# The tail of a fused attention, MLP and mixture kernel issued from one written plan, with its maximum and low halves on other engines

## The chip, the cores and the metric

The kernel runs on one core of one Trainium2 chip. The metric is the device time in microseconds (us), the median of several executions. The core's engines work side by side, each through its own queue in order, and wait for one another by semaphores: TensorE (PE, matrix products), VectorE (DVE), ScalarE (ACT), GpSimd (POOL) and SyncE (SP, which here only issues DMAs).

## The reference

```python
# attention: b=4, 8 heads, 576 rows, head size 64; phi(x) = [exp(xW-m), exp(m-xW)]
kv = einsum(phi(k), v);  x = (phi(q) @ kv) / (phi(q) @ sum(phi(k)) + 1e-6)   # -> x: 2304 x 512
# MLP, 512 -> 2048 -> 512
h = np.maximum(x @ w_in, 0.0)
x = h * h @ w_out
# mixture, E=4 experts, 512 -> 1024 -> 512
p = domain_probs / (domain_probs.sum(-1, keepdims=True) + 1e-09)
for e in range(E):
    h = np.maximum(x @ w1[e], 0.0)
    out += p[:, e:e + 1] * (h @ w2[e])
```

All is computed to float32 accuracy. TensorE multiplies in a shorter format, so each operand is split into a high half (a rounded copy) and a low half (the operand minus its high half), and each product is three matmuls: high by low, low by high, high by high.

## The kernel before, in words

The 2304 tokens are cut by batch row b into blocks of 512 tokens; the 64 tokens left over of each of the four rows make one block of 256, the rest.

The first part is issued from a written plan: functions put steps into a list with `at(time, ...)`, and the list, sorted by time, sets the order of every engine's queue. The times only order; nothing waits for a clock. It computes attention for all rows, and the MLP for rows 0 and 1 (`Unit`, lines 515 and 562 on PE). Attention's outputs for rows 2, 3 and the rest go to DRAM (`put_x`, `put_rest`).

The second part, from line 723 on, here the tail, is written as ordinary code without a plan, and the framework orders it. Its three passes are the MLP on rows 2, 3 and the rest (8 groups of hidden features), the mixture on rows 0 and 1 (16 groups), and the mixture on rows 2, 3 and the rest (16 groups). One group of a pass is a unit:

- `Weights` loads 256 columns of the first matrix (`f`) and 256 rows of the second (`f2`), forms four sums of blocks on POOL (line 801), and splits all into high halves on ACT and low halves on POOL (line 83).
- `hidden_pair` computes the hidden activations of two blocks with seven block products in place of eight (Strassen's scheme): px, py, pz and pv are PSUM banks, and DVE combines them into u4, c and u2 (line 868). Each product is 6 matmuls of 512 columns (line 860), 42 in all.
- `act_mlp` or `act_mix` turns the four hidden tiles (px, u4, c, u2) into a high half gh and a low half gl. In a mixture, ACT writes gh = relu. For px, in PSUM, DVE forms gl as max(px, 0) - gh in one instruction (line 845). For the other three, in SBUF, POOL first takes the maximum in place (line 849) and then subtracts (line 83).
- `hidden_rest`, in passes with the rest, adds 24 matmuls of 256 columns (line 897) into one bank pa.
- `out_mlp` or `out_mix` computes the outputs: 8 banks pa of 6 matmuls of 512 columns (line 912 or 929); for the rest 4 banks of 6 matmuls of 256 columns in the MLP, 2 of 6 by 512 in a mixture. DVE adds each bank to the accumulators `x2` (line 917 or 935).

`flush` puts the outputs of a unit behind the next unit's seven products in the pass without a rest, and behind the unit's own `hidden_rest` in the others. `Operands` prepares a pass's left operands: four sums or differences on DVE (T3, T1, T2, T4) and seven splits. Their low halves are named ol.

Of the kernel before, what the change touches and what calls it, by code (L numbers as in the profile page):

```python
# [21 lines left out]
def fused_kernel(  # L22
# [44 lines left out]
    actx = ExitStack()  # L67
# [37 lines left out]
    def load_probs():  # L105
# [22 lines left out]
        "g": actx.enter_context(tc.tile_pool(name="g", bufs=4)),  # L128
        "w": actx.enter_context(tc.tile_pool(name="w", bufs=3, side="right")),
    }  # L130
    xpool = actx.enter_context(tc.tile_pool(name="x", bufs=2))
# [440 lines left out]
    def new_x2(b):  # L572
        n = MAIN if b < B else NL
        pool = ypool if b < 2 else zpool
        x2[b] = pool.tile([P, KD, n], F32, name=f"x2_{b}")
# [140 lines left out]
    with tc.manual_schedule():  # L716
        for _, _, fn, args in sorted(plan, key=lambda x: x[:2]):
            fn(*args)
    cctx.close()
    actx.close()  # L720


    def left(name, bufs=1):
        return ctx.enter_context(tc.tile_pool(name=name, bufs=bufs, reuse_waits="tile"))

    ps_t = ctx.enter_context(tc.tile_pool(name="ps_t", bufs=4, space=bass.MemoryType.PSUM, reuse_waits="tile"))
    pools["ps"] = ps_t
    w2pool = left("w2", 2)
    gpool = left("g2", 6)
    upool = left("sums", 6)  # L730
    opool = left("operands")
    zpool = left("z")
    fpool = left("f", 4)
    w1pool = left("w1", 2)
    lpool = left("rest")

    def f_tile(*shape):
        return fpool.tile([P, *shape], F32, tag="f", name="f")

    def u_tile():  # L740
        return upool.tile([P, 512], F32, tag="u", name="u")

    for b in (2, 3, 4):
        new_x2(b)

    HK = KD // 2
    PRODUCTS = ("B11", "T2", "T1", "T3", "B21", "B22", "T4")

    class Operands:


        def __init__(self, b0, b1, engs):
            (b11, b12), (b21, b22) = ([x2[b][:, k : k + HK] for b in (b0, b1)] for k in (0, HK))
            self.h, self.l = {}, {}
            t = {"B11": b11, "B21": b21, "B22": b22, "T1": b12}
            for name, a, b in (("T3", b22, b12), ("T1", b12, b11), ("T2", b22, "T1"), ("T4", b21, "T2")):
                if name not in t:
                    t[name] = f_tile(HK, MAIN)
                sub(nc.vector, t[name], a, t.get(b, b) if isinstance(b, str) else b)
            for name, eng in zip(PRODUCTS, engs):  # L760
                self.h[name], self.l[name] = (
                    opool.tile([P, HK, MAIN], F32R, tag=x + name, name=f"o{x}") for x in "hl"
                )
                split(nc.scalar, eng, self.h[name], self.l[name], t[name])

    def load_x():
        for b in (2, 3):
            for k in range(0, KD, HK):
                nc.sync.dma_start(out=x2[b][:, k : k + HK], in_=kept["x", b][:, k : k + HK])
        nc.sync.dma_start(out=x2[B], in_=kept["xL"])  # L770

    class Rest:


        def __init__(self):
            self.h, self.l = (lpool.tile([P, KD, NL], F32R, tag=f"rest{n}", name="rest") for n in "hl")
            split(nc.scalar, nc.vector, self.h, self.l, x2[B])
# [3 lines left out]
    FIRST_OF = ((1, 2), (0, 3))  # L781

    class Weights:
        def __init__(self, first_srcs, second_srcs, rest):
            w1 = w1pool.tile([P, 2, 8, HK, P], F32R, tag="w1", name="w1")
            self.h, self.l = h, l = w1[:, 0], w1[:, 1]
# [4 lines left out]
            for s in (0, 1):  # L791
                nc.sync.dma_start(out=f[:, 3 * s], in_=first_srcs[1][:, s * HK : (s + 1) * HK])
# [216 lines left out]
```

## Time and profile before

| what | value |
|---|---|
| median of 3 runs | 1495.78 us (1494.72 to 1496.09) |
| the profiled execution's own time | 1497.08 us |
| its span, first to last instruction | 1495.3 us |
| busy, share of the span | PE 93%, POOL 69%, DVE 59%, ACT 39% |
| PE from 460.8 us on | 976.6 us busy in 1029.6 us |
| median against the profiled execution's own time | 1.30 us less |

All engines run through the whole span, so the busiest one, PE, is the one to ask first. A busy PE is not a PE at its peak: the granted clock (1.00 is 2.4 GHz, 0.50 is 1.2 GHz) stands beside its busy time in the windows below.

### The profile page before, as it was taken

The page shows a single profiled execution, that of the slowest core. Times are in us where ns is not written, and L with a number is a line of the kernel's source. Part 1 is how long each engine was busy: PE and PEld are TensorE (multiplying, and loading weights), DVE is VectorE, ACT ScalarE, POOL GpSimd, SP SyncE. Part 2 cuts the span into 40 slices and gives each one's busy share as a digit, 9 for nine tenths or more (in the row PEclk, how much of TensorE's full clock was granted, in tenths as well). Part 3 has the DMA queues.
Part 4 walks back from the last instruction along what each step waited for, and adds up shares of the span by engine and source line. Part 5 has one row for each costly group of instructions (what it writes and reads, how often), then busy time and mean ns, then how long its engine had stood idle before and what let it go on. Part 6 is the DMA issues. An engine that isn't in the chain of part 4 may idle for free.

```text
span 1495.3 us, 18786 instructions
## 1 busy us (share of the span) xinstructions
PE 1390.7 (93%) x6906; PEld 1152.2 (77%) x6906; DVE 884.3 (59%) x1208; ACT 585.7 (39%) x1034; POOL 1024.7 (69%) x734
## 2 busy tenths in 40 slices
PE   7899999999885999998999999995999999999998
PEld 6777887887764888786888888874787878878876
DVE  5888798999874355665544554573344444444444
ACT  4677776766543434243332222232122231221210
POOL 2566776767659657648998888868467577576652
PEclk8999999999996999998999999997999999999999
DMA  5334334444332101001111111102101011111102
GB/s 129 85 90 104 106 104 134 132 127 116 95 128 85 43 28 31 27 29 57 57 57 58 57 57 54 32 29 78 64 29 57 29 29 57 28 35 51 29 1 71
DMA packets 136940, 97.43 MB, mean 65 GB/s; under 512 B 70288, under 2 KB 113424, under 8 KB 136848
## 3 DMA queue, kind: packets, MB, share of 16 engines
q1 hardware_dynamic: 136848, 96.23, 22.3%
q8 instruction: 55, 0.90, 0.2%
q14 instruction: 37, 0.30, 0.1%
HBM read 80.32 MB, written 15.80 MB: 64 GB/s over the span
## 4 chain that ended last, share of the span: by engine, by line
PE 62%; POOL 14%; DVE 13%; issue 5%; ACT 2%; DMA 2%; SPq 1%; POOLq 0%; DVEq 0%; ACTq 0%
PE pa L929 21%; PE px L860 6%; PE pz L860 6%; PE pv L860 6%; POOL gl L83 6%; PE pa L912 5%; POOL u L849 4%; PE py L860 3%; PE ph L515 3%; PE pm L325 2%; POOL f L801 2%; PE pm L562 2%; POOL w L83 1%; DVE top L456 1%; PE pm L359 1%
## 5 line engine op out<-in xcount | busy, mean ns | idle before, releaser
L935 DVE SCALAR_TENSOR_TENSOR x<-pa,prob,x 128x512 f32<-128x512 f32 x270 | 202.0, 750 | 188.4 <-PE pa L929 188.4
L849 POOL TENSOR_SCALAR u<-u 128x512 f32<-128x512 f32 x96 | 143.9, 1499 | 172.3 <-ACT gh L843 172.3
L929 PE MATMUL pa<-w2h,gl 128*128 128x512 f32 x576 | 228.6, 397 | 34.8 <-POOL gl L83 34.2
L83 POOL TENSOR_TENSOR gl<-u,gh 128x512 fp32r<-128x512 f32 x136 | 181.3, 1340 | 76.0 <-PE pa L912 56.0
L929 PE MATMUL pa<-w2l,gh 128*128 128x512 f32 x576 | 226.1, 393 | 0.0
L929 PE MATMUL pa<-w2h,gh 128*128 128x512 f32 x576 | 225.6, 392 | 0.0
L83 POOL TENSOR_TENSOR w<-f,w 128x1024 fp32r<-128x1024 f32 (+1 forms) x80 | 184.4, 2322 | 4.8 <-ACT w L78 4.6
L929 PEld LDWEIGHTS pa<-w2h,gl 128*128 128x128 f32 x576 | 109.2, 190 | 64.9 <-POOL gl L83 41.5
L929 PEld LDWEIGHTS pa<-w2h,gh 128*128 128x128 f32 x576 | 109.1, 189 | 23.2
L929 PEld LDWEIGHTS pa<-w2l,gh 128*128 128x128 f32 x576 | 109.4, 190 | 21.6
L801 POOL TENSOR_TENSOR f<-f 128x256 f32<-128x256 f32 x160 | 120.8, 775 | 7.0 <-DMA f<-in_moe_w_dram 1.5
L83 POOL TENSOR_TENSOR q<-qf,q 128x1024 fp32r<-128x1024 f32 (+1 forms) x64 | 96.0, 1510 | 36.2 <-DVE q L80 35.4
L874 ACT ACTIVATE u<-px 128x512 f32<-128x512 f32 x40 | 24.0, 599 | 234.4 <-PE px L860 234.4
L83 POOL TENSOR_TENSOR w2l<-f,w2h 128x1024 fp32r<-128x1024 f32 x40 | 96.4, 2410 | 18.1 <-ACT w2h L78 18.1
L860 PE MATMUL px<-oh,w 128*128 128x512 f32 x320 | 99.6, 393 | 8.9 <-POOL w L83 8.9
L78 ACT ACTIVATE w<-f 128x1024 fp32r<-128x1024 f32 (+1 forms) x80 | 78.2, 1009 | 73.5 <-POOL f L801 43.9
L860 PE MATMUL pz<-oh,w 128*128 128x512 f32 x320 | 98.8, 390 | 0.0
L860 PE MATMUL pv<-oh,w 128*128 128x512 f32 x320 | 98.5, 389 | 0.0
L868 DVE TENSOR_TENSOR u<-py,u 128x512 f32<-128x512 f32 x40 | 27.7, 691 | 104.1 <-PE py L860 104.1
L843 ACT ACTIVATE gh<-u 128x512 fp32r<-128x512 f32 x96 | 60.2, 628 | 68.3 <-issue 33.1
L912 PE MATMUL pa<-gl,w2h 128*128 128x512 f32 (+1 forms) x192 | 72.2, 376 | 15.7 <-POOL gl L83 13.1
L469 POOL TENSOR_TENSOR wf<-wf,top 128x512 f32<-128x512 f32 x32 | 43.5, 1358 | 58.2 <-DVE wf L464 54.1
(151 smaller groups left out, 3365.6 us busy)
## 6 DMA issues: line engine op xcount, KB each, us to landing
f<-in_moe_w_dram SPq DMA_DIRECT2D x96, 256.0 KB
raw<-in_moe_w_in_dram SPq DMA_DIRECT2D x16, 512.0 KB
raw<-in_moe_w_out_dram SPq DMA_DIRECT2D x16, 512.0 KB
f<-in_moe_w_dram SPq DMA_DIRECT2D x64, 128.0 KB
rec<-one SPq DMA_DIRECT2D x32, 144.0 KB
qk<-in_q_dram SPq DMA_DIRECT2D x32, 128.0 KB
qk<-in_k_dram SPq DMA_DIRECT2D x32, 128.0 KB
va<-in_v_dram SPq DMA_DIRECT2D x32, 128.0 KB
```

Source lines behind the costliest of these rows:

```text
L78: nc.scalar.activation(out=dst, in_=src, func=AF.Copy)
L83: eng.tensor_tensor(out=dst, in0=a, in1=b, op=ALU.subtract)
L325: nc.tensor.matmul(pk[:VW, : 2 * NF], lhsT=a, rhs=m, start=i == 0, stop=i == len(ops) - 1)
L469: nc.gpsimd.tensor_tensor(out=self.dst, in0=self.dst, in1=f32(self.top), op=ALU.add)
L515: nc.tensor.matmul(p[:, :n], lhsT=a, rhs=m, start=i == 0, stop=i == len(ops) - 1)
L801: nc.gpsimd.tensor_tensor(out=sums[:, s], in0=a, in1=b, op=op)
L843: nc.scalar.activation(out=gh, in_=src, func=AF.Relu)
L849: nc.gpsimd.tensor_scalar_max(src, src, 0.0)
L860: nc.tensor.matmul(p, lhsT=a[:, s, k], rhs=m[name][:, k], start=start and k == 0 and m is o.l, skip_group_check=not start, stop=stop and k ...
L912: nc.tensor.matmul(p[:, :n], lhsT=a, rhs=m, start=i == 0, stop=i == len(ops) - 1)
L929: nc.tensor.matmul(p, lhsT=a, rhs=m, start=i == 0, stop=i == len(ops) - 1)
L935: nc.vector.scalar_tensor_tensor(out=o, in0=p, scalar=pe, in1=o, op0=ALU.mult, op1=ALU.add)
```

## The change

The tail is issued from the same written plan as the first part. `plan_tail` puts every step of the three passes into the list, and the former functions are split into small steps (`Weights.hi`, `Act.lo`, `MixOut.mm` and so on). Its steps begin at plan time 404.7, among the last steps of the first part (whose last are at 437.9).

Beside the order, these things differ. The maximum on POOL is gone: in a mixture all low halves are formed on DVE by the one instruction that px already had, with u4, c and u2 read from SBUF. In the MLP the low halves stay on POOL. Of the seven low halves of the operands, five are on DVE in the MLP pass and four in the mixtures, against four before; the others stay on POOL. The outputs of a unit stand right behind its own hidden products in every pass, those of the second row of the pair (j = 1, which reads c and u4) first, and in each bank the matmul that reads a low half comes third and sixth instead of first and fourth. There are 5 buffers `f` instead of 4, 4 buffers `u` instead of 6; the first-layer weights have two pools, of which one opens late. The load of the mixture's probabilities is issued in the first unit.

```diff
-    def act_mix(src, in_psum):
-        gh, gl = g_tiles()
-        nc.scalar.activation(out=gh, in_=src, func=AF.Relu)
-        if in_psum:
-            nc.vector.scalar_tensor_tensor(
-                out=gl, in0=src, scalar=0.0, in1=f32(gh), op0=ALU.max, op1=ALU.subtract
-            )
-        else:
-            nc.gpsimd.tensor_scalar_max(src, src, 0.0)
-            sub(nc.gpsimd, gl, src, f32(gh))
+        def lo(self):
+            if self.square:
+                sub(nc.gpsimd, self.gl, self.r, f32(self.gh))
+            else:
+                nc.vector.scalar_tensor_tensor(
+                    out=self.gl, in0=self.src, scalar=0.0, in1=f32(self.gh), op0=ALU.max, op1=ALU.subtract
+                )
...
-                ops += [(gl, w.h2[:, i]), (gh, w.l2[:, i]), (gh, w.h2[:, i])]
+                ops += [(gh, w.l2[:, i]), (gh, w.h2[:, i]), (gl, w.h2[:, i])]
...
+        def relu(self, src):
+            self.src = self.r = src()
+            if self.square:
+                if self.in_psum:
+                    self.r = tail["u"].tile([P, 512], F32, tag="u", name="u")
+                nc.scalar.activation(out=self.r, in_=self.src, func=AF.Relu)
+            else:
+                self.hi()
...
+    PT, RT, OT = 1.37, 2.85, 1.37
+    EARLY_AT, LATE_AT, TAIL_AT = 404.7, 438.2, 433.0
+    def plan_weights(w, t, square):
+        at(t - 6, w.load)
+        at(t + 7, w.load2)
+        at(t + 0.9, w.sums)
+        at(max(t + 1.95, LATE_AT + 0.3), w.hi)
+        at(max(t + 3.5, LATE_AT + 1.5), w.lo)
+        at(max(t + 4.2, LATE_AT + 1.6), w.hi_sums)
+        at(t + (15.0 if square else 6.6), w.lo_sums)
+        at(t + 11.3, w.hi2)
+        at(t + (17.6 if square else 12.0), w.lo2)
+    def plan_pair(u, t, square):
+        for i, (b, name, start) in enumerate((
+            ("x", "B11", True), ("y", "T2", True), ("z", "T1", True), ("v", "T3", True),
+            ("z", "B22", False), ("x", "B21", False), ("v", "T4", False),
+        )):
+            at(t + i * PT, u.product, b, name, start)
+        at(t + PT, u.first)
+        at(t + 2 * PT, u.add, "u2", "y", "u2")
+        at(t + 3 * PT, u.add, "u4", "z", "u2")
+        at(t + 4 * PT, u.add, "u4", "v", "u4")
+        at(t + 5 * PT, u.add, "c", "z", "u2")
+        at(t + 7 * PT, u.add, "u2", "v", "u2")
+        steps = ("relu", "sq", "hi", "lo") if square else ("relu", "lo")
+        times = {
+            "u4": (4.5, 5.1, 5.6, 6.1), "c": (5.5, 6.0, 6.6, 7.1), "x": (6.1, 6.6, 7.05, 7.6), "u2": (7.5, 8.0, 8.5, 9.0),
+        } if square else {
+            "u4": (4.5, 5.02), "c": (5.5, 6.0), "x": (6.1, 6.6), "u2": (7.5, 8.0),
+        }
...
+    def plan_operands(o, t):
+        for i, n in enumerate(("T3", "T1", "T2", "T4")):
+            at(t - 3 + 0.3 * i, o.sum, n)
+        for i, n in enumerate(PRODUCTS):
+            at(t + 11.35 + 1.1 * i, o.hi, n)
+            at(t + (12.4 + 1.3 * i if i < 4 else 16.9 + 2.7 * (i - 4)), o.lo, n, nc.vector if i < 4 else nc.gpsimd)
+    def plan_out(us, t, length):
+        for i, o in enumerate(us):
+            at(t + i * length, o.mm)
+            at(t + (i + 1) * length, o.add)
+        return t + len(us) * length
...
+            if square:
+                for b in pair:
+                    for k in (0, HK):
+                        at(EARLY_AT + 0.1, o.load, b, k)
+                at(EARLY_AT + 0.2, rest.load)
+                for i, n in enumerate(("T3", "T1", "T2", "T4")):
+                    at(412 + 1.2 * i, o.sum, n)
+                for i, n in enumerate(PRODUCTS):
+                    at(413 + 1.6 * i, o.hi, n)
+                    at(416 + 1.6 * i, o.lo, n, nc.vector if i not in (4, 6) else nc.gpsimd)
+            else:
+                plan_operands(o, before[0])
+            if rest:
+                at(LATE_AT + 0.2 if square else t - 15, rest.make)
...
+                if before is None:
+                    at(EARLY_AT + 0.05, w.load)
+                    at(EARLY_AT + 0.3, w.load2)
+                    for i, f in enumerate((w.sums, w.hi, w.lo, w.hi_sums, w.lo_sums, w.hi2, w.lo2)):
+                        at(408 + 2 * i, f)
+                else:
+                    plan_weights(w, *before)
...
+                for j in (1, 0):
+                    if square:
+                        t = plan_out([MlpOut(u, j, pair[j], MAIN, d, ends[0]) for d in range(KD)], t, OT)
+                    else:
+                        t = plan_out([MixOut(u, j, pair[j], i, group[0], *ends) for i in range(NJ)], t, OT)
```

The first place is PE in a unit of the second mixture pass, where the 24 matmuls of the rest end and the outputs begin. Before, and then after:

```order
L897 MATMUL pa_10173<-rest_9870,w1_10062 128x256 x2
L929 MATMUL pa_10202<-w2h_10064,gl_10139 128x512
L929 MATMUL pa_10202<-w2l_10063,gh_10138 128x512
L929 MATMUL pa_10202<-w2h_10064,gh_10138 128x512
L929 MATMUL pa_10202<-w2h_10064,gl_10153 128x512
L929 MATMUL pa_10202<-w2l_10063,gh_10152 128x512
L929 MATMUL pa_10202<-w2h_10064,gh_10152 128x512
```

```order
L943 MATMUL pa_10134<-rest_9707,w1_9876 128x256 x2
L988 MATMUL pa_10170<-w2l_9963,gh_10119 128x512
L988 MATMUL pa_10170<-w2h_9962,gh_10119 128x512
L988 MATMUL pa_10170<-w2h_9962,gl_10120 128x512
L988 MATMUL pa_10170<-w2l_9963,gh_10104 128x512
L988 MATMUL pa_10170<-w2h_9962,gh_10104 128x512
L988 MATMUL pa_10170<-w2h_9962,gl_10105 128x512
```

Before, the first bank reads the low half of px (gl_10139) in its first matmul and that of u2 (gl_10153), the last of the four tiles, in its fourth; after, it reads the low half of c (gl_10120) in its third and that of u4 (gl_10105) in its sixth.

The second place is POOL in a unit of the second mixture pass. Before, and then after:

```order
L849 TENSOR_SCALAR u_12536<-u_12536 128x512
L83 TENSOR_TENSOR gl_12591<-u_12536,gh_12590 128x512
L849 TENSOR_SCALAR u_12537<-u_12537 128x512
L83 TENSOR_TENSOR gl_12596<-u_12537,gh_12595 128x512
L849 TENSOR_SCALAR u_12535<-u_12535 128x512
L83 TENSOR_TENSOR gl_12601<-u_12535,gh_12600 128x512
L83 TENSOR_TENSOR w2l_12715<-f_12719,w2h_12716 128x1024
L83 TENSOR_TENSOR w1_12918<-f_12921,w1_12918 128x1024
L83 TENSOR_TENSOR w1_12918<-f_12922,w1_12918 128x1024
```

```order
L821 TENSOR_TENSOR f_12071<-f_12027 128x256 x2
L821 TENSOR_TENSOR f_12071<-f_12071,f_12027 128x256
L821 TENSOR_TENSOR f_12071<-f_12027,f_12071 128x256
L83 TENSOR_TENSOR w1_12087<-f_12027,w1_12087 128x1024
L83 TENSOR_TENSOR w1_12087<-f_12071,w1_12087 128x1024
L83 TENSOR_TENSOR w2l_12174<-f_12126,w2h_12173 128x1024
```

POOL keeps only the weights; the three pairs of maximum and subtraction left it, and three subtractions with maximum stand on DVE.

The third place is DVE where the first part ends: L570 (after: L571) adds the MLP outputs of rows 0 and 1, L83 rows make the operands of rows 2 and 3. Before, and then after:

```order
L570 TENSOR_TENSOR x2_0_101<-pm_5269,x2_0_101 128x512
L83 TENSOR_TENSOR x2_3_5358<-x2_3_5358,x2_2_5357 128x1024
L570 TENSOR_TENSOR x2_0_101<-pm_5276,x2_0_101 128x512
L570 TENSOR_TENSOR x2_1_102<-pm_5290,x2_1_102 128x512
L83 TENSOR_TENSOR f_5368<-x2_3_5358 128x1024
L570 TENSOR_TENSOR x2_1_102<-pm_5297,x2_1_102 128x512
L83 TENSOR_TENSOR f_5370<-x2_2_5357,f_5368 128x1024
L570 TENSOR_TENSOR x2_1_102<-pm_5306,x2_1_102 128x512
L570 TENSOR_TENSOR x2_1_102<-pm_5313,x2_1_102 128x512
```

```order
L83 TENSOR_TENSOR f_5346<-x2_2_5273,f_5340 128x1024
L83 TENSOR_TENSOR ol_5348<-x2_2_5273,oh_5327 128x1024
L83 TENSOR_TENSOR ol_5355<-f_5340,oh_5342 128x1024
L571 TENSOR_TENSOR x2_0_101<-pm_5329,x2_0_101 128x512
L83 TENSOR_TENSOR ol_5363<-x2_3_5274,oh_5351 128x1024
L83 TENSOR_TENSOR ol_5368<-f_5324,oh_5357 128x1024
L83 TENSOR_TENSOR ol_5383<-x2_2_5273,oh_5370 128x1024
L571 TENSOR_TENSOR x2_1_102<-pm_5372,x2_1_102 128x512
L571 TENSOR_TENSOR x2_1_102<-pm_5385,x2_1_102 128x512
```

The sums and all five low halves of the operands now stand ahead of the last four additions of the first part, of which two are shown; before, three of the four low halves on DVE came behind all of its additions.

## Rows read from the trace of the kernel before

**Rows 1.** The page's first part: busy time, share of the span, instructions.

```profile
PE 1390.7 (93%) x6906; PEld 1152.2 (77%) x6906; DVE 884.3 (59%) x1208; ACT 585.7 (39%) x1034; POOL 1024.7 (69%) x734
```

**Rows 2.** Busy time by stretches of the tail; behind the engines granted clock, DMA share, GB/s.

```profile
448.00:460.80 12.80, 0.80 (x1) 0.29 (x1) 9.09 (x7) 4.95 (x5) 11.41 (x7) 0.56 0.27 82
460.80:467.00 6.20, 6.17 (x15) 4.84 (x16) 0.69 (x1) 1.55 (x2) 6.20 (x5) 0.53 0.36 97
460.80:699.90 239.10, 220.97 (x1080) 186.23 (x1081) 119.07 (x167) 88.13 (x133) 158.31 (x107) 0.94 0.13 41
699.90:1048.60 348.70, 330.64 (x1456) 273.08 (x1455) 177.28 (x236) 101.20 (x136) 300.45 (x216) 0.97 0.17 53
1048.60:1490.40 441.80, 425.02 (x2027) 353.88 (x2025) 198.67 (x274) 99.69 (x139) 271.08 (x191) 1.00 0.13 39
```

**Rows 3.** The chain of waits: start us, us, what; one output stretch per unit.

```profile
567.76 10.50 PE pa L912 x45
...
594.53 5.51 PE pa L912 x23
...
823.97 10.88 PE pa L929 x48
...
844.37 10.88 PE pa L929 x48
...
1368.54 10.54 PE pa L929 x45
...
1395.76 10.54 PE pa L929 x45
```

**Rows 4.** Timeline of PE in a unit of the second mixture pass.

```profile
1391.15 3.04 PE L897 MATMUL pa<-rest,w 128*128 128x256 f32 x24
1394.02 0.40 PE L929 MATMUL pa<-w2h,gl 128*128 128x512 f32 x1
...
1395.76 0.50 PE L929 MATMUL pa<-w2h,gl 128*128 128x512 f32 x1 [0.88 <-POOL gl L83]
```

**Rows 5.** Timeline of POOL there.

```profile
1394.41 1.29 POOL L83 TENSOR_TENSOR gl<-u,gh 128x512 fp32r<-128x512 f32 x1
```

**Rows 6.** Timeline of PE between the two mixture passes.

```profile
1037.79 0.80 PE L929 MATMUL pa<-w2h,gl 128*128 128x512 f32 x1 [17.38 <-POOL gl L83]
```

**Rows 7.** Lines 843, 845, 935 and 83: duration in ns, minimum/median/maximum, then first and last start.

```profile
L843 ACT ACTIVATE gh<-u x96: 612/632/636, 707.4 to 1471.0; 128x512 fp32r<-128x512 f32 x96
...
L845 DVE SCALAR_TENSOR_TENSOR gl<-px,gh x32: 680/692/694, 707.5 to 1468.2; 128x512 fp32r<-128x512 f32 x32
...
L935 DVE SCALAR_TENSOR_TENSOR x<-pa,prob,x x270: 735/751/753, 743.8 to 1490.6; 128x512 f32<-128x512 f32 x135
...
L83 POOL TENSOR_TENSOR w<-f,w x80: 1835/2399/3489, 458.4 to 1427.6; 128x1024 fp32r<-128x1024 f32 x64, 128x768 fp32r<-128x768 f32 x16
```

**Rows 8.** Line 835; DVE's timeline; the chain at the same moment on POOL.

```profile
L835 DVE TENSOR_TENSOR u<-u x24: 676/693/2694, 470.9 to 677.9; 128x512 f32<-128x512 f32 x24
...
470.93 2.69 DVE L835 TENSOR_TENSOR u<-u 128x512 f32<-128x512 f32 x1 [1.13 <-ACT u L834]
...
470.66 2.42 POOL w L83
```

**Rows 9.** Timeline of PE, then of DVE, at the end of a product py.

```profile
857.80 0.39 PE L860 MATMUL pz<-ol,w 128*128 128x512 f32 x1
...
858.10 0.69 DVE L868 TENSOR_TENSOR u<-py,u 128x512 f32<-128x512 f32 x1 [2.07 <-PE py L860]
```

**Rows 10.** Timelines of PE and DVE where the tail begins.

```profile
440.73 0.50 PE L562 MATMUL pm<-gl,wh 128*128 128x512 f32 x1 [1.38 <-POOL gl L83]
...
460.83 1.22 PE L860 MATMUL px<-oh,w 128*128 128x512 f32 x2 [8.86 <-POOL w L83]
...
437.86 1.69 DVE L83 TENSOR_TENSOR f<-x 128x1024 f32<-128x1024 f32 x1 [0.57 <-DMA f<-w_i]
...
449.26 4.50 DVE L83 TENSOR_TENSOR ol<-f,oh 128x1024 fp32r<-128x1024 f32 x2
```

More of the change, by code (lines that the diff above doesn't have):

```diff
@@ L766, in load_x, with left, open_early @@
[L766 to L770, printed above, removed]
+    HK = KD // 2
+    PRODUCTS = ("B11", "T2", "T1", "T3", "B22", "B21", "T4")
+    tail = {}
+    def left(name, bufs=1, **how):
+        tail[name] = ctx.enter_context(tc.tile_pool(name=name, bufs=bufs, reuse_waits="tile", **how))
+    def open_early():
+        cctx.close()
+        xctx.close()
+        actx.close()
+        left("o", 4, space=bass.MemoryType.PSUM)
+        for name, bufs in (("z", 1), ("f", 5), ("w1a", 1), ("operands", 1), ("w2", 2), ("u", 4)):
+            left(name, bufs)
+        for b in (2, 3, 4):
+            new_x2(b)
@@ new lines, in fused_kernel, with __init__, hidden, source @@
+    class RestUnit:
+        def __init__(self, w, o, square):
+            self.w, self.o, self.act = w, o, Act(square, True)
+        def hidden(self):
+            w, o = self.w, self.o
+            self.p = p = obank()
+            for i in range(2):
+                q = p[:, i * NL : (i + 1) * NL]
+                for kk in range(KD):
+                    s, k = FIRST_OF[i][kk // HK], kk % HK
+                    for j, (a, m) in enumerate(((w.h, o.l), (w.l, o.h), (w.h, o.h))):
+                        nc.tensor.matmul(
+                            q, lhsT=a[:, s, k], rhs=m[:, kk], start=kk + j == 0, stop=kk == KD - 1 and j == 2
+                        )
+        def source(self):
+            return self.p
+        def gs(self, _):
+            return [[x[:, i * NL : (i + 1) * NL] for x in (self.act.gh, self.act.gl)] for i in range(2)]
@@ L921, in out_mix, with add, __init__, mm @@
-    def out_mix(w, g, b, n, e, is_first, is_last):
-        for t in range(n // P):
-            p = bank()
+                nc.tensor.matmul(self.p[:, :n], lhsT=a, rhs=m, start=i == 0, stop=i == len(ops) - 1)
+        def add(self):
+            x, p = x2[self.b][:, self.d, : self.n], self.p[:, : self.n]
+            if self.is_first:
+                nc.scalar.activation(out=x, in_=p, func=AF.Copy)
+            else:
+                nc.vector.tensor_tensor(out=x, in0=p, in1=x, op=ALU.add)
+    class MixOut:
+        def __init__(self, u, j, b, t, e, is_first, is_last):
+            self.u, self.j, self.b, self.t, self.e, self.ends = u, j, b, t, e, (is_first, is_last)
+        def mm(self):
+            self.p, w, t = obank(), self.u.w, self.t
@@ L982 @@
+    plan_tail()
+    with tc.manual_schedule():
+        for _, _, fn, args in sorted(plan, key=lambda x: x[:2]):
+            fn(*args)
 _INS = ["q", "k", "v", "w_phi", "moe_w_in", "moe_w_out", "moe2_domain_probs", "moe2_w1", "moe2_w2"]
```

338 lines of the change are left out of this document (168 added, 170 removed).

## The prediction

> **What bounds the kernel now.** I read the page's busy shares first: PE is busy 93% of the span [rows 1], so no gain can come from another engine's work as such, only from PE's idle and slow time. Next I cut the tail at the first products of its passes [rows 2]: from 460.8 to 699.9 us the MLP, to 1048.6 the first mixture, to 1490.4 the second. PE is busy 221, 331 and 425 us of 239, 349 and 442, at granted clocks of 0.94, 0.97 and 1.00. To turn this into excess I need what a unit costs when nothing waits.
>
> The chain of waits shows 48 output matmuls of 512 columns in 10.88 us [rows 3], a slot of 0.2267 us. A pair of blocks takes 42 + 48 = 90 slots, 20.40 us, and the units of the first mixture are just that far apart (823.97 to 844.37 [rows 3]): there is nothing to win in a steady unit of that pass. The 24 half-width matmuls of the rest take 1394.02 - 1391.15 = 2.87 us [rows 4]. So a unit of the second mixture should cost 102 slots + 2.87 = 25.99 us; it takes 27.21 [rows 3]. An MLP unit should cost 20.40 + 2 x 2.87 = 26.14 us; it takes 26.77 [rows 3].
>
> The whole tail without a wait: 8 x 26.14 + 16 x 20.40 + 16 x 25.99 = 209.1 + 326.4 + 415.9 = 951.4 us. It takes 1490.4 - 460.8 = 1029.6 us, so 78.2 us are excess. By pass (the MLP's last rest outputs, 2.87 us, fall behind 699.9): 32.9 in the MLP, 19.4 in the first mixture, 25.9 in the second. What the excess is: in the second mixture 16 x 1.22 = 19.5 us. In each unit PE stops after three output matmuls for POOL's low half of u2 (0.88 us idle [rows 4]), which POOL finishes at 1394.41 + 1.29 = 1395.70 [rows 5], behind two more maximum-and-subtract pairs. In the first mixture nearly all is one stop of 17.38 us before the last outputs, again for POOL [rows 6]. In the MLP it is short stops and stretches at half clock.
>
> **The change part by part.**
>
> *PE's work.* The same matmuls in another order: 951.4 us stay.
>
> *Low halves on DVE, outputs of c and u4 first.* POOL loses its maximum and three subtractions per mixture unit. On DVE each new instruction should take what the one for px takes, 0.69 us [rows 7], since a square that reads only SBUF also has a median of 0.69 [rows 8]. DVE per first-mixture unit: 5 sums x 0.69 [rows 9] + 4 low halves x 0.69 + 8 additions x 0.75 [rows 7] = 12.2 of 20.4 us; it doesn't become the bound.
> But the outputs now follow the hidden products at once, so latency counts. I count from a unit's first product, seven products of 1.36. The bank of c is full at 5 x 1.36 = 6.80, and DVE starts 0.30 after the next product has begun [rows 9], at 7.10. Its queue: sum of c to 7.8, low half of u4 to 8.5; ACT meanwhile makes c's high half (0.63 [rows 7]) by 8.5; low half of c to 9.2. PE reads it in the third output matmul, at 9.52 + 0.45 = 9.97. Slack 0.7 us: no stop in the first mixture. In passes with the rest the slack is 2.87 us more. The low half of u2 is read four banks (5.44 us) after that. So the 19.5 us of the second mixture go to 0.
>
> *MLP units.* Squares stay on DVE, low halves on POOL. With 4 buffers u instead of 6, the relu of the rest, a fifth tile, must wait until POOL has read u2's. I follow that chain with the same durations and POOL's 1.29 per subtraction [rows 5]: POOL is done with u2 at 14.9 if nothing collides, 15.8 if DVE's square of u2 waits out a subtraction of POOL; relu and square of the rest end 1.4 later, at 16.3 to 17.2. The bank they free is due at 9.52 + 2.87 + 3 x 1.36 = 16.47. So 0 to 0.7 us per unit. I take 0.7, 5.6 in all, as POOL also carries the weights here.
>
> *The start of the tail.* This part does not gain. Before, the first part's last matmuls waited for POOL until 440.73, and the tail's products ran from 460.83 [rows 10]. After, the weights' loads stand ahead of the loads of x in SP's queue, and those behind the same stores as before, so I put the first difference of x at 438.5 (before 437.86 [rows 10], right behind a DMA). DVE's queue then holds three sums of up to 1.69 us [rows 10] and two additions ahead of T2's high half (445); behind that high half on ACT stands the first part's last gh. So that gh comes near 447, POOL's gl near 449, and the last four output banks of the first part, which waited until 440.7 before, start 8 us later. The fourth of them needs a bank that DVE frees only behind one more sum and five low halves of up to 2.25 us (4.50 for two [rows 10]): 445 + 1.7 + 5 x 2.25 = 458. After its 6 matmuls the first product starts at 460, between 453 (x early, no collisions) and 467 (each low half behind one of POOL's). Against 460.8 that is a gain of 0.8.
>
> *Changes of pass.* Operands are now made within the preceding unit. DVE's four sums, 4 x 1.69 = 6.8 us, sit between the last outputs; the next unit's py, pz sums are then about 2 us late for the bank that product B22 accumulates into. Later in the unit four low halves of 2.25 us stand among output additions, 9 us in which some three additions fall due, and the four output banks cover about 3 us of lag (three banks of 1.36 less 0.30 and an addition): I get 4.6 us into the first mixture (the square of the rest is late too) and 2 into the second, together with the sums 10.6. Bounds: 3 (all covered) and 22 (twice that, two stops then also falling to half clock). The 17.38 us stop goes, since POOL's queue there holds only weights and three low halves.
>
> *Clock.* Where PE idled from 448 to 460.8 the granted clock over the stretch was 0.56, and 0.53 over the 6.2 us after [rows 2]: half speed, 1.2 GHz, for some 6 us, a cost of about 3. Idle times of 1 to 2 us in the second mixture left it at 1.00 [rows 2]. So I add none for short stops.
>
> *Two inputs from SBUF.* DVE's new low halves read two tensors in SBUF while POOL works on weights. One such square on DVE, begun 0.27 us after a subtraction of POOL, took 2.69 us, until just after POOL was done [rows 8]; an instruction of DVE with one input in PSUM never took more than 0.753 in 270 [rows 7]. So a low half of c that meets POOL's split of weights (2.40 [rows 7]) is up to 2.4 late, and 2.4 - 0.7 = 1.7 us of PE are lost. I count on POOL being through: both its splits of the first layer start with ACT's high half, about 3.3 into the unit, and take 2 x 2.25, to 7.8, when the low half of u4 begins. The Trainium skill says in GPSIMD Engine Reference, section Specifications, that GpSimd shares its SBUF interface with VectorE and contends with instructions that have two SBUF inputs; the trace agrees by the rows just named, and by that rule every collision counts, which is the second case below.
>
> **Sum.** 460.0 + 951.4 + 5.6 + 10.6 + 4.9 (from 1490.4 to the span's end, 1495.3) = 1432.5 us of span. The profiled execution's own time is 1.8 above its span and the median 1.3 below that time: 1433 as a median.
>
> **The rivals.**
> 1. *As above*, 1433, of its own 1417 to 1450 (start 7 either way, passes 3 to 22).
> 2. *Collisions in each unit of the first mixture.* POOL's splits slip by some tenths, and c's low half waits: 16 x 1.7 = 27 us, 1460. For it: the slack is 0.7 us against splits of up to 3.49 [rows 7]. Against: they end just ahead of it in the order.
> 3. *Starts and passes are covered.* x lands early, banks cover DVE's lag: 7 + 7 + 4 less, 1415.
> 4. *Starts and passes are worse.* Every operand low half on DVE waits for one on POOL: start at 467, passes 22, then 1452; a clock lost twice gives 1458.
> 5. *Slower than before.* The immediate outputs stop PE long enough in each unit to lose the clock. The stop in a first-mixture unit would be 2.5 us (a late c low half plus a further collision) and half clock behind it costs 3: 5.5 x 16 = 88 us, 1521. It decides from (1495.8 - 1433) / 16 = 3.9 us a unit. For it: such outputs do wait in the trace when nothing stands between [rows 6]. Against: 0.88 us of idle did not drop the clock [rows 2, 4].
> 6. *No change*, the tail being PE's work anyway: that needs 78 us of excess to come back elsewhere.
>
> **How the numbers follow.** Chances: 54% for 1, 16% for 2, 14% for 3, 11% for 4, 4% for 5, 1% for 6. The range from 1410 to 1464 holds nearly all of 2 to 4 and the likely case; beyond it lie 5 and 6 and the tails. About 0.2% is what a measurement of this kernel can tell from no change, 3 us. Faster by more than that: 95%; within it 1%; slower 4%.
>
> **What would show it.** Right: units of 20.4, 26.0 and 26.1 to 26.9 us between first products; no wait of PE for POOL's gl in the second mixture; first product near 460; stops of 2 to 5 us at the two changes of pass and none of 17. Wrong: PE waiting for DVE's gl at the third output matmul in the first mixture, with gl rows of 1.5 us and more beside POOL's splits; PE waiting for DVE's additions in the MLP's outputs by more than 1 us; a first product beyond 467; granted clocks under 1.00 inside the passes.

## The result, and the profile after

The changed kernel takes 1431.62 us (median of 4 runs, 1431.59 to 1432.34) against 1495.25 for the kernel before on the same chip: a ratio of 0.9577, 95% interval 0.9561 to 0.9594. The forecast was 1433, between 1410 and 1464. The profiled execution's span is 1429.8 us, the granted clock over it 0.983.

The page's first part, to be laid beside [rows 1]:

```profile
PE 1370.9 (96%) x6906; PEld 1144.9 (80%) x6906; DVE 953.4 (67%) x1305; ACT 580.9 (41%) x1034; POOL 753.6 (53%) x541
```

POOL has lost 271 us of work, DVE has gained 69, and PE's share has gone from 93 to 96%. The tail by stretches, cut at the first products of its passes, with the stretch ahead of it (columns as in [rows 2]):

```profile
444.00:458.60 14.60, 9.91 (x25) 7.51 (x26) 12.95 (x8) 3.86 (x5) 12.90 (x8) 0.62 0.27 74
458.60:674.75 216.15, 212.10 (x1105) 181.26 (x1104) 122.48 (x177) 86.30 (x132) 138.82 (x94) 1.00 0.12 38
674.75:1007.35 332.60, 328.01 (x1443) 270.23 (x1441) 206.60 (x278) 99.16 (x136) 160.89 (x117) 1.00 0.17 52
1007.35:1424.90 417.55, 417.55 (x2017) 353.09 (x2015) 233.64 (x324) 100.80 (x141) 152.88 (x106) 1.00 0.14 45
```

Against the pure costs of the prediction (209.1, 326.4 and 415.9 us) the passes now carry 7.1, 6.2 and 1.7 us of excess, where they carried 32.9, 19.4 and 25.9. Between first products a unit of the MLP takes 26.20 us (five of the eight, a sixth 26.39), one of the first mixture 20.40 (14 of 16), one of the second 26.02. What is left sits at the start and at the two changes of pass. PE's timeline there, its longest stops:

```profile
444.19 0.79 PE L563 MATMUL pm<-gl,wh 128*128 128x512 f32 x1 [11.35 <-POOL gl L83]
...
455.81 0.80 PE L563 MATMUL pm<-gl,wh 128*128 128x512 f32 x1 [4.49 <-DVE x L571]
...
458.54 0.63 PE L913 MATMUL px<-ol,w 128*128 128x512 f32 x1
...
669.03 0.50 PE L966 MATMUL pa<-gh,w2l 128*128 128x512 f32 x1 [1.68 <-DVE x L973]
...
685.97 0.50 PE L988 MATMUL pa<-w2h,gl 128*128 128x512 f32 x1 [1.05 <-DVE gl L891]
...
1005.46 0.50 PE L988 MATMUL pa<-w2l,gh 128*128 128x512 f32 x1 [2.80 <-DVE x L997]
```

The waits of 0.88 us in each unit of the second mixture and of 17.38 us between the mixtures [rows 4, 6] are gone. At the start the stops are longer than before [rows 10]. There DVE's timeline shows what its low halves cost while POOL makes low halves too (the second fence is POOL's):

```profile
433.31 1.64 DVE L83 TENSOR_TENSOR f<-x 128x1024 f32<-128x1024 f32 x1 [3.82 <-DMA x<-x]
...
441.80 1.22 DVE L83 TENSOR_TENSOR ol<-x,oh 128x1024 fp32r<-128x1024 f32 x1
442.93 2.29 DVE L83 TENSOR_TENSOR ol<-f,oh 128x1024 fp32r<-128x1024 f32 x1
...
445.75 2.81 DVE L83 TENSOR_TENSOR ol<-x,oh 128x1024 fp32r<-128x1024 f32 x1
448.49 3.39 DVE L83 TENSOR_TENSOR ol<-f,oh 128x1024 fp32r<-128x1024 f32 x1
451.80 3.36 DVE L83 TENSOR_TENSOR ol<-x,oh 128x1024 fp32r<-128x1024 f32 x1
455.08 1.87 DVE L571 TENSOR_TENSOR x<-pm,x 128x512 f32<-128x512 f32 x3
```

```profile
447.44 3.35 POOL L83 TENSOR_TENSOR ol<-x,oh 128x1024 fp32r<-128x1024 f32 x1
450.76 3.32 POOL L83 TENSOR_TENSOR ol<-f,oh 128x1024 fp32r<-128x1024 f32 x1
```

The same instruction takes DVE 1.22 us alone, 2.3 to 2.8 where an instruction of POOL stands in its way for a part, and 3.4 where the two engines go in turn; POOL's then takes 3.3 instead of 2.4. The addition that frees PE's bank stands behind all five, at 455.08.

### The profile page after: what moved, and what is told of

Its sections match the earlier page's. It is cut to its first block, busy times and chain, and to the rows that moved or that the text cites. A ratio compares the mean times of both kernels' runs of the same rounds, so it can differ in the third digit from the quotient of the medians.

```text
span 1429.8 us, 18665 instructions
## 1 busy us (share of the span) xinstructions
PE 1370.9 (96%) x6906; PEld 1144.9 (80%) x6906; DVE 953.4 (67%) x1305; ACT 580.9 (41%) x1034; POOL 753.6 (53%) x541
## 4 chain that ended last, share of the span: by engine, by line
PE 67%; DVE 12%; ACT 3%; issue 2%; POOL 1%; DMA 0%; SPq 0%; DVEq 0%; ACTq 0%; POOLq 0%
PE pa L988 27%; PE pz L913 7%; PE px L913 7%; PE pv L913 7%; PE pa L966 7%; PE pa L943 4%; PE py L913 4%; DVE ol L83 2%; PE ph L516 2%; DVE x L571 1%; DVE wf L477 1%; DVE top L460 1%; PE pm L563 1%; DVE kf L83 1%; DVE mx L231 1%
## 5 line engine op out<-in xcount | busy, mean ns | idle before, releaser
L83 POOL TENSOR_TENSOR w<-f,w 128x1024 fp32r<-128x1024 f32 (+1 forms) x80 | 184.0, 2318 | 288.6 <-ACT w L78 288.6
L988 PE MATMUL pa<-w2h,gl 128*128 128x512 f32 x576 | 224.6, 390 | 1.1 <-DVE gl L891 1.1
L83 POOL TENSOR_TENSOR w2l<-f,w2h 128x1024 fp32r<-128x1024 f32 x40 | 96.1, 2403 | 142.1 <-ACT w2h L78 142.1
L885 ACT ACTIVATE gh<-u 128x512 fp32r<-128x512 f32 x136 | 85.8, 631 | 161.4 <-DVE u L923 151.3
L83 POOL TENSOR_TENSOR q<-qf,q 128x1024 fp32r<-128x1024 f32 (+1 forms) x64 | 96.4, 1517 | 32.0 <-DVE q L80 31.3
L923 DVE TENSOR_TENSOR u<-pz,u 128x512 f32<-128x512 f32 x80 | 55.3, 691 | 51.3 <-PE pz L913 50.4
L891 DVE SCALAR_TENSOR_TENSOR gl<-u,gh 128x512 fp32r<-128x512 f32 x96 | 72.0, 760 | 24.9 <-ACT gh L885 23.4
L78 ACT ACTIVATE w<-f 128x1024 fp32r<-128x1024 f32 (+1 forms) x80 | 76.9, 1009 | 2.9 <-POOL f L821 2.9
L83 POOL TENSOR_TENSOR gl<-u,gh 128x512 fp32r<-128x512 f32 x40 | 53.6, 1360 | 41.8 <-ACT gh L885 41.8
```

The source lines that it names most:

```text
L78: nc.scalar.activation(out=dst, in_=src, func=AF.Copy)
L83: eng.tensor_tensor(out=dst, in0=a, in1=b, op=ALU.subtract)
L885: nc.scalar.activation(out=self.gh, in_=self.r, func=AF.Copy if self.square else AF.Relu)
L891: nc.vector.scalar_tensor_tensor(out=self.gl, in0=self.src, scalar=0.0, in1=f32(self.gh), op0=ALU.max, op1=ALU.subtract)
L923: nc.vector.tensor_tensor(out=self.u[out], in0=self.p[a], in1=self.u[b], op=ALU.add)
L988: nc.tensor.matmul(self.p, lhsT=a, rhs=m, start=i == 0, stop=i == len(ops) - 1)
```

## The experiments

All ratios below are to the kernel before, as run beside the experiment.

**Where the first product's time comes from: the probabilities' load.** In the kernel before, the framework had placed the load of the mixture's probabilities near the program's start, though the source has it in the tail. DVE's timeline of the kernel before has a wait there that the prediction missed:

```profile
23.19 0.23 DVE L115 TENSOR_REDUCE psum__82<-prob 128x18 f32<-128x72 f32 x1 [4.67 <-DMA prob<-in_moe_domain_probs_dram]
```

In the changed kernel the load is planned at LATE_AT + 4, and the first part runs 6 to 7 us earlier from there on. Two kernels move it alone, back in the changed kernel (`e1_probs_early`) and away in the kernel before (`e2_before_probs_late`); `load_probs` is cut in two at its reduction, the second half named `norm_probs`:

```diff
+    PROBS = 12.9, 12.95                    # e1, from the kernel after
...
-        at(LATE_AT + 4, load_probs)
+        at(PROBS[0], load_probs)
+        at(PROBS[1], norm_probs)
...
+    at(300, load_probs)                    # e2, from the kernel before: in the first part's plan
+    at(330, norm_probs)
...
-    load_probs()
```

> The kernel after, with the load of the mixture's probabilities and its normalisation put back to where the kernel before had them: eight transfers on SP at the start and the four small instructions of DVE behind the first exponentials. Theory (the kernel before lost time there: DVE waited 4.67 us for those transfers at 18.5 us, and everything of the first part ran 6 to 7 us later): the first part is later by 4 to 7 us, the first product px comes near 464 instead of 458.54, and the time is 1436 to 1438 us. Rival (the wait at the start is made up for before the tail, and the earlier first difference of x in the kernel after has another cause): first product within 1 us of 458.5, 1431 to 1433 us.

> The kernel before, with that load moved away from the start (transfers planned at 300 us of the first part, normalisation at 330, where nothing waits for it). Theory: first product px near 454.5 instead of 460.83, time 1489 to 1490.5 us, so 5 to 6.4 us of the change's gain are this move alone. Rival: 1494 to 1496 us, no gain, because the start of the tail waits for something else.

Measured: 1435.5 us (0.9599, interval 0.9586 to 0.9612) and 1488.98 us (0.9959, 0.9947 to 0.9972). In the first, DVE again waits for the transfers, 5.63 us; the first difference of x begins at 439.74 instead of 433.31, and the first product px at 463.77 instead of 458.54. In the second PE's px, held up until 460.83 before [rows 10], starts again at 454.07. So this move alone is worth 6.5 us in the kernel before, an effect of the rewriting that has nothing to do with the tail's work. In the changed kernel it is worth less: put back, it makes the first product 5.2 us later and the kernel 3.9 longer, as the first unit gives 1.0 of the difference back (28.52 us against 29.54).

**The engine move and the written order apart.** `e4_before_lows_on_dve` keeps the old order and moves only the low halves; `e3_lows_on_pool` keeps the new order and moves them back; `e11_before_both` is e4 with e2's edit.

```diff
-        if in_psum:                                # e4, act_mix before
-            nc.vector.scalar_tensor_tensor(...)
-        else:
-            nc.gpsimd.tensor_scalar_max(src, src, 0.0)
-            sub(nc.gpsimd, gl, src, f32(gh))
+        nc.vector.scalar_tensor_tensor(out=gl, in0=src, scalar=0.0, in1=f32(gh), op0=ALU.max, op1=ALU.subtract)
+            elif not self.in_psum:                 # e3, Act.lo after
+                nc.gpsimd.tensor_scalar_max(self.src, self.src, 0.0)
+                sub(nc.gpsimd, self.gl, self.src, f32(self.gh))
```

> The kernel before, its order kept, with the low halves of u4, c and u2 in the mixtures on DVE in one instruction each and no maximum on POOL. Theory (the move of the engine alone takes the stops of the mixtures away: 1.22 us in each of 16 units of the second, 17.38 us at the change between the two): 1495 - 19.5 - 14 to 17 = 1459 to 1462 us; the MLP and the start stay as they are. Rival (in the old order the moved low halves collide with POOL's weights, or the stops are handed to DVE): 1475 to 1495 us.

> The kernel after, its order kept, but maximum and low half of u4, c and u2 in the mixtures back on POOL as before (1.57 and 1.26 us each from start to start, 2.83 a tile). Theory (the new order can't do without the move to DVE): in a first-mixture unit POOL is free of the weights at 7.2 us, done with u4 at 10.0 and with c at 12.9, and PE needs c's low half at 9.97: a stop of 2.9 us in each of 16 units, 46 us; in the second mixture the rest covers 2.87 and 0.9 us a unit is left, 14 us. Sum 1432 + 60 = 1492; up to 1525 if stops of 2.9 us also cost the granted clock, PE naming POOL's gl as what it waits for. Rival (the order alone brings the gain, POOL has time enough): 1432 to 1440 us.

> The kernel before with both single moves that gained: the probabilities' load away from the start and the low halves of u4, c and u2 on DVE in one instruction. Theory (the two gains, 6.5 and 35.3 us, lie at different places and add): 1452 to 1456 us, so that 20 to 24 us of the change's 64 are left for the written order itself, most of them in the MLP pass. Rival (they overlap, because an earlier tail meets other waits): 1457 to 1465 us.

Measured: e4 1460.23 us (0.9769, 0.9754 to 0.9784), e11 1454.81 (0.9733, 0.971 to 0.9757), e3 1515.34 (1.0126, 1.0111 to 1.0141). In e4 the units of the second mixture come down to 26.02 us without any change of order, and in place of the 17.38 us stop PE waits 5.3 us for DVE's additions. The two single moves together give 40 us. The remaining 23 belong to all else that was changed: the order, and with it the buffers and the engines of the operands' low halves, which no run here takes apart. They lie in the MLP: in e11 it takes 238.8 us at a granted clock of 0.94 (216.2 at 1.00 in the changed kernel), and its outputs still wait for POOL's gl (12.9 us in 9 waits, the longest 5.0). e3 is slower than the kernel before. PE's and POOL's timelines in one of its first-mixture units:

```profile
816.48 0.79 PE L991 MATMUL pa<-w2h,gl 128*128 128x512 f32 x1 [2.75 <-POOL gl L83]
817.07 0.63 PE L991 MATMUL pa<-w2l,gh 128*128 128x512 f32 x1
817.50 0.63 PE L991 MATMUL pa<-w2h,gh 128*128 128x512 f32 x1
```

```profile
813.60 1.49 POOL L891 TENSOR_SCALAR u<-u 128x512 f32<-128x512 f32 x1
815.16 1.26 POOL L83 TENSOR_TENSOR gl<-u,gh 128x512 fp32r<-128x512 f32 x1
```

The stop is 2.75 us of idle PE where 2.9 were expected; behind it the output matmuls start 0.43 us apart instead of 0.23, half clock. Of the 14 units between the first and the last, six take 23.4 us, 3.0 more than without a stop and all of it at full clock, and eight 24.8 to 26.3. So the new order without the new engine loses 84 us, and the old order with it gains 35: the order needs the move, not the other way round.

**DVE and POOL on SBUF, by themselves.** `e7_collide` moves one instruction of ACT, so that POOL's subtraction for the weights' sums ends late instead of 0.4 us ahead of DVE's low half:

```diff
-        at(max(t + 4.2, LATE_AT + 1.6), w.hi_sums)
+        at(max(t + (4.2 if square else 6.3), LATE_AT + 1.6), w.hi_sums)
```

> The kernel after with one thing moved in the mixtures: ACT makes the high half of the weights' sums after that of u4 instead of before, so that POOL's subtraction of 2.4 us runs from 8.0 to 10.4 us of a unit instead of ending at 7.2, 0.4 us before DVE's low half of u4. Theory (DVE with two inputs from SBUF waits out an instruction of POOL): c's low half, due to start at 8.4 to 9.3, ends near 11.0 instead of 9.1, PE needs it at 9.97: a stop of about 1.1 us in the units of the first mixture and none in the second, 16 to 18 us, 1447 to 1450 us; rows of the low half of 2 us and more. Rival (no such sharing; DVE takes 0.69 us beside POOL): 1431 to 1433 us.

Measured: 1449.06 us (0.9689, 0.9673 to 0.9704), 17.4 above the changed kernel. The timelines of DVE, POOL and PE in one unit:

```profile
748.33 2.59 DVE L891 SCALAR_TENSOR_TENSOR gl<-u,gh 128x512 fp32r<-128x512 f32 x1 [0.21 <-ACT gh L885]
```

```profile
747.86 2.51 POOL L83 TENSOR_TENSOR w<-f,w 128x1024 fp32r<-128x1024 f32 x1 [3.15 <-ACT w L78]
```

```profile
750.98 0.50 PE L988 MATMUL pa<-w2h,gl 128*128 128x512 f32 x1 [1.01 <-DVE gl L891]
```

POOL is done at 750.37, DVE 0.55 us later: nearly all of its 0.69 us of work was done after POOL. PE waits for DVE's gl 16 times, 16.5 us in all, and a unit takes 21.70 us instead of 20.40: 1.30 more, as the two matmuls beside the stop start 1.40 us apart instead of 0.23 and the next one 0.34. This is the prediction's second case, produced on purpose, and the changed kernel runs 0.4 us beside it in each unit of that pass but the first (POOL done at 744.58, DVE's low half begun at 744.95).

**The order of the outputs.** `e8_outputs_in_order` makes the mixtures' first block's outputs first, as before (u2's steps are planned earlier so that they stand ahead of them):

```diff
-        at(t + 7 * PT, u.add, "u2", "v", "u2")
+        at(t + (7 if square else 6.65) * PT, u.add, "u2", "v", "u2")
...
-            "x": (6.1, 6.6), "u2": (7.5, 8.0),
+            "x": (6.1, 6.6), "u2": (6.7, 6.9),
...
-                for j in (1, 0):
+                for j in ((1, 0) if square else (0, 1)):
```

> The kernel after with the mixtures' outputs of the first block (x and u2) ahead of those of the second (u4 and c), as the kernel before had them. Theory (the order of outputs is what leaves time for the last low half): u2's low half ends 11.8 us into a unit, and PE would need it at 10.65: a stop of 1.15 us in each unit of the first mixture, none in the second where the rest lies between, 18 us, 1449 to 1451 us, PE naming ACT's high half or DVE's low half. Rival (the order makes no difference because banks and DVE leave more time than that): 1431 to 1434 us.

Measured: 1454.06 us (0.9721, 0.9706 to 0.9735), 22 above. PE now waits in each first-mixture unit for u2's high half; a unit takes 21.79 us (743.23 to 765.02 between first products), 1.39 more, where 1.15 was expected:

```profile
754.42 0.50 PE L988 MATMUL pa<-w2l,gh 128*128 128x512 f32 x1 [0.82 <-ACT gh L885]
```

**What was left: the start and the changes of pass.** `e5_start` reorders the start alone: the first part's last relu, halves and additions ahead of the operands' work on their engines, and all operand low halves and the first weights' low halves on DVE. `e6_passes` moves all operand low halves of the changes of pass to DVE, in another order. The excerpts show the main lines of each:

```diff
-                    at(413 + 1.6 * i, o.hi, n)                                          # e5
-                    at(416 + 1.6 * i, o.lo, n, nc.vector if i not in (4, 6) else nc.gpsimd)
+    LAST = ({"add": (38.2, 36.6, 34.72, 38.9)}, {"g_hi": (11.9, 15.28), "g_lo": (16.4, 16.51),
+        "out": (20.8, 20.6, 20.7, 20.9), "add": (23.9, 22.9, 23.4, 24.4)})   # the first part's last unit
+    FIRST_OPERANDS = {   # sum, high half, low half; all low halves on nc.vector
+        "T3": (415, 415.5, 420), "T1": (416, 416.2, 419), "T2": (416.7, 416.9, 418.2), "T4": (417.6, 417.7, 423),
+        "B11": (None, 412.5, 413.5), "B22": (None, 415.1, 421), "B21": (None, 415.2, 422)}
...
-            at(t - 3 + 0.3 * i, o.sum, n)                                               # e6
...
-            at(t + (12.4 + 1.3 * i if i < 4 else 16.9 + 2.7 * (i - 4)), o.lo, n, nc.vector if i < 4 else nc.gpsimd)
...
+            at(t - 5 + 0.9 * i, o.sum, n)
+        for i, n in enumerate(("T3", "B11", "T2", "T1", "B22", "B21", "T4")):
...
+            at(t + 12.4 + 1.4 * i, o.lo, n, nc.vector)
```

> The kernel after with only the order of the start of the tail changed: the first part's last relu, high and low halves and its last additions stand ahead of the operands' work on ACT, POOL and DVE; the first weights' low halves and all seven operand low halves are on DVE, so that POOL does nothing with two inputs from SBUF while DVE makes them. Theory (the 11.35 and 4.49 us stops of PE and the collisions of DVE and POOL are only order): the first part's last 24 matmuls follow without a stop and end near 438.5, the first product px comes between 440 and 445 instead of 458.54, low halves of DVE take 1.2 us, unit 0 loses up to 3 us: 1411 to 1418 us. Rival (the start is bound by the arrival of x at 433.3 and by the amount of DVE's work, whatever its order): first product beyond 452, 1425 us or more.

> The kernel after with only the changes of pass rewritten: all seven operand low halves on DVE (three were on POOL), T3 first, the four sums some 2 us earlier, the rest's split for the second mixture one unit earlier, where output additions have slack. Theory (the 10.6 us of the two changes come from DVE's low halves waiting out POOL's): low halves of 1.2 us, the stop of 2.80 us before the second mixture goes, 2 to 5 us are left of 10.6: 1423 to 1427 us. Rival (it is the amount of DVE's work among the output additions that costs, so seven low halves cost more than four): 1431 to 1438 us.

Measured: e5 1419.69 us (0.9498, 0.9479 to 0.9517), e6 1432.38 (0.9574, 0.9558 to 0.959), no gain. In e5 the first part's last matmuls follow with one stop of 1.96 us and the first product comes at 438.34, 20 us earlier; but the first unit then takes 37.9 us (29.5 in the changed kernel), because DVE's sums over the products' banks now stand behind its last operands (4.75 us) and POOL's weights still collide with them. Of the 20 us, 12 are left where the second unit begins. In e6 most low halves take 1.21 us, and the stop of 2.80 us goes, but DVE has three more of them among the output additions: the change into the first mixture got 4.8 us longer (28.09 and 32.75 us for the last two units of the MLP and 21.28 for the first of the mixture, against 26.20, 29.29 and 21.79), the one into the second 1.9 shorter. The time is the one the rival gave, but its reason, the amount of DVE's work, doesn't hold: e10, below, has the same seven low halves on DVE at this place, three of them behind the last output additions, and loses 2.0 us there.

`e9_both` puts those sums ahead of the last operands, POOL's weights behind them, and splits the work of the changes anew; `e10_refined` then takes up what it left:

```diff
+    NEXT_OPERANDS = {   # high half, low half, engine, from the preceding unit's start; e10
+        True: {"T3": (11.35, 12.4, V), "B11": (12.45, 13.8, V), "T2": (13.55, 15.2, V), "T1": (14.65, 20.0, V),
+               "B22": (15.75, 26.3, V), "B21": (16.85, 26.9, V), "T4": (17.95, 24.5, V)},
+        False: {"T3": (11.35, 12.4, V), "B11": (12.45, 13.8, V), "T2": (13.55, 15.2, V), "T1": (14.65, 16.6, V),
+               "B22": (15.75, 18.0, V), "B21": (20.4 + 1.5, 20.4 + 1.6, G), "T4": (20.4 + 1.55, 20.4 + 1.65, G)}}
...
+    # FIRST_OPERANDS: "T4": (438.2, 438.3, 439.5), "B22": (None, 415.1, 437.2), "B21": (None, 415.2, 438.6)
...
-            at(LATE_AT + 0.2 if square else t - 15, rest.make)
+            at(LATE_AT + 0.02 if square else t - 28, rest.hi)
+            at(t + 6.9 if square else t - 28, rest.lo)
...
-        at(t + 0.9, w.sums)
+        at(t + (9.8 if first else 0.9), w.sums)     # first: the weights made in the MLP's first unit
```

> The start of e5_start refined (sums of the hidden products' banks and the rest's split no longer behind the last operands on DVE; POOL's weights of the second unit and its second-layer weights after the low halves, so that POOL has no two-input work beside them), and the changes of pass once more: into the first mixture seven low halves on DVE with a pause while POOL does its two weights, into the second mixture five on DVE and the last two on POOL after the pass has begun. Theory (both limits are the one shared way to SBUF plus DVE's queue order, and spreading the two engines' two-input work in time frees it): unit 0 of the MLP takes 30 to 32 us instead of 37.9, 6 to 8 us; the changes of pass cost 2 to 5 us instead of 10.6; 1405 to 1410 us. Rival (DVE's total amount at these places is the limit, as the run with only the passes changed suggested): 1416 to 1422 us.

> The start of e9_both with its three remaining long waits taken up: the rest's high half goes ahead of T4's on ACT and its low half ahead of the squares on DVE (PE waited 3.79 us for it), the second unit's sums on POOL go between the low halves of c and x, and ACT makes their high half after two of its first output copies (PE waited 3.00 us there); the first second-layer low half goes to DVE. In the change into the first mixture the low halves of B22, B21 and T4 go behind the last output additions; the change into the second stays as in e9_both. Theory (what e9_both lost in the MLP's first unit, 40.6 us where e5_start took 37.9, was the queue order behind the operands, and the change into the second mixture kept its gain of 4.4 us): first unit 33 to 35 us, 1410 to 1414 us. Rival (the shared way to SBUF is full there in any order, so each move hands the wait on): first unit 37 to 41 us, 1417 to 1421 us.

Measured: e9 1419.27 us (0.9489, 0.9475 to 0.9504), no better than e5 as a whole and in the rival's range: its change into the second mixture gained 4.4 us, the one into the first lost 1.7, and its first unit lost 2.7, waiting 3.79 us for the rest's low half and 3.00 for an output copy behind POOL's sums on ACT. e10, with these two waits taken up, 1410.57 us (0.9438, 0.9418 to 0.9459): 84 us below the kernel before and 21 below the changed one. DVE's timeline of e10 where the tail begins shows the operands at their own price, 1.22 us each, while POOL does nothing:

```profile
445.25 1.22 DVE L83 TENSOR_TENSOR ol<-f,oh 128x1024 fp32r<-128x1024 f32 x1
446.39 1.22 DVE L83 TENSOR_TENSOR ol<-x,oh 128x1024 fp32r<-128x1024 f32 x1
447.52 1.22 DVE L83 TENSOR_TENSOR ol<-f,oh 128x1024 fp32r<-128x1024 f32 x1
448.66 0.68 DVE L934 TENSOR_TENSOR u<-py,u 128x512 f32<-128x512 f32 x1
```

Its first unit takes 31.7 us (33 to 35 expected, 37 to 41 by the rival), its two changes of pass cost 2.0 and 1.6, and PE is busy 927.6 of the 930 us from 475 to 1405.

## Why the prediction was right, step by step

**The total** (1433 against 1431.62) is right, and the mechanism that carries it, the units at their pure cost, is the one in the trace. That it is right to 1.4 us is luck: the terms err both ways, by up to 5 us. Three of the prediction's signs of being wrong showed once each, all at the changes of pass: PE waited 1.68 us for DVE's addition in the MLP's outputs (669.03), 1.05 us for DVE's gl at a third output matmul (685.97), and the clock fell before the second mixture.

**Units at their pure cost, low halves on DVE.** Right, and the largest part: 20.40 and 26.02 us, POOL waited for in no steady unit. The latency count held as well: in a unit from 737.35, c's low half ended at 746.43, 9.08 in (9.2 counted), and is read at 9.97. e7 shows what the slack was worth, and e3 and e4 what the move was.

**The MLP.** 5.6 us were taken for the chain of the u buffers; it cost nearly nothing (26.20 against 26.14 in the steady units). The first unit lost 3.4 us instead, behind the start; with 0.6 for the rest the term is 4.0. The last unit's stops belong to the change of pass.

**The start.** The step "the tail's products start at 460, a gain of 0.8" came out at 458.54, by two errors that nearly cancel. The first difference of x began at 433.31, not 438.5: the reading took the kernel before's first part as unchanged and missed the 4.67 us wait for the probabilities. e1 and e2 show this term; with the load put back, the difference begins at 439.74. And from there to the first product it took 25.2 us, not 21.5. Some 2 us of this are the five low halves on DVE, which took 13.1 us in all, the last two 3.4 each in turn with POOL's, where 2.25 each was taken: the fourth case's collisions, in part. Another 1.4 are the last six matmuls behind them, which ran at half clock (0.43 us apart). The chain itself, gh behind the operands on ACT, then POOL's gl, then the bank behind the low halves, is the one in the trace. e5, where it is put in another order and POOL's share of the low halves moved to DVE, starts the product 20 us earlier; its first unit gives 8.4 of them back.

**The changes of pass.** 10.6 us predicted, 10.6 measured, but this agreement is luck too, as they are split otherwise: into the first mixture 3.1 + 1.4 = 4.5 (6.6 predicted), into the second 4.8 + 1.3 = 6.1 (4). In the second the stop of 2.80 us was followed by half clock (slots of 0.43 us from 1006.50 to 1009), which the sum left out. It leaned on idle times of 1 to 2 us in the second mixture of the kernel before, at a clock of 1.00. That was misread: the stops there are 0.81 to 1.14 us, but for one of 3.50 us (1067.55), behind which the clock is 0.50 and the matmuls 0.43 us apart until 1070.7.

**The rivals.** Collisions in the units of the first mixture did not happen in 15 of the 16, by 0.4 us. In the first unit there was one, DVE's row of u4's and c's low halves beside POOL's of the weights:

```profile
682.46 3.46 DVE L891 SCALAR_TENSOR_TENSOR gl<-u,gh 128x512 fp32r<-128x512 f32 x2
```

```profile
680.55 4.21 POOL L83 TENSOR_TENSOR w<-f,w 128x768 fp32r<-128x768 f32 x2
```

It made the stop of 1.05 us shown above, and is the 1.4 us counted with the change into the first mixture. Made to happen in all units by e7, the collisions cost 17 us more (27 predicted for all 16: a unit loses 1.30, not 1.7). The fifth case, immediate outputs that stop PE and lose its clock, is near what e3 does, 1515 us against 1521, but by another road: there the late low half of c is POOL's and not DVE's, half clock follows in eight of 14 units only, and some 14 of its 84 us lie in the second mixture. The case as it stands, a stop of 2.5 us for DVE's low half in each unit of the first mixture, no run shows.

## What to carry to other kernels

Before the work of DVE and POOL is laid side by side, count which of DVE's instructions read two tensors from SBUF, and plan these for times when POOL has nothing to do: an engine that looks idle is no help while it holds the other one up. In an engine's queue, put the few instructions that free a bank or feed the next matmul ahead of the bulk work prepared for later; at this kernel's start that, with the low halves taken off POOL, was worth 12 us (e5). And when a rewritten part takes over a load, look where the old program had really issued it, since a gain may lie far from the change.

## What the hardware showed that was not expected

Where DVE and POOL both work on tensors in SBUF, the turns they take cost both sides. DVE's subtraction of 128x1024 took 1.22 us alone and 3.4 in turn with POOL's, which took 3.3 instead of 2.4; POOL's four sums of a weight took 2.94 us alone (751.81 in the changed kernel) and 6.71 beside DVE's low halves (445.01 in e5). An instruction of DVE on 128x512 with a bank as one input kept its 0.67 to 0.75 us beside POOL throughout. Two inputs from SBUF are not the whole condition, though: in the changed kernel one small instruction with a single input tensor, the TENSOR_SCALAR of 128x18 at 471.93 (line 116), took 1.29 us beside POOL's subtractions of 1.3, and 0.17 in the kernel before, where it began ahead of POOL (25.66).

The clock's answer to an idle time is not fixed by its length. Three neighbouring units of e3, with stops of 2.75, 2.72 and 2.73 us at the same place and the same work, by windows from first product to first product (columns as in [rows 2]):

```profile
803.60:829.86 26.26, 23.51 (x91) 18.86 (x90) 10.13 (x14) 5.65 (x8) 17.56 (x13) 0.87 0.14 41
829.86:854.89 25.03, 22.31 (x92) 17.99 (x90) 10.14 (x14) 5.65 (x8) 17.57 (x13) 0.93 0.14 43
854.89:878.33 23.44, 20.71 (x91) 16.82 (x90) 10.13 (x14) 5.65 (x8) 17.61 (x13) 1.00 0.14 45
```

The granted clock is 0.87, 0.93 and 1.00, and the first two units take 2.8 and 1.6 us more than the third for it. In e7, with a stop of 1.0 us in each of 15 units and of 1.4 in the last, the clock over that pass (675.00 to 1026.60) is 1.00. What decides it these runs don't settle.

The first part's length varies from run to run: the profiled executions of e5, e9 and e10, whose first parts are alike in order up to 400 us, have their first products at 438.34, 442.93 and 444.29 us; e6, with the changed kernel's own start, has it 1.9 us earlier than the changed kernel. Differences inside the tail were therefore read from first product to first product, and the times from medians.
